# A gMLP layer rebuilt around one z2 tile, a spatial weight in four quarters and hand-over of memory tile by tile

## The chip, the cores and the metric

The kernel runs on one core of one Trainium2 chip. The metric is the device time of one execution in microseconds (us); every quoted time is the median of several executions, and a profiled execution gives the trace from which all durations below are read. TensorE does the matrix products, VectorE, ScalarE and GpSimd the element-wise work, and SyncE's queue (SP) most of the transfers.

## The reference, cut to what matters

Four layers follow each other: attention (A), gMLP (B), attention, gMLP. The change concerns B alone.

```
S, D, F = 2048, 576, 4608;  Fh = F // 2 = 2304
z  = gelu(x @ w_in)                    # x: layer-normalised, w_in: D x F
z1 = z[..., :Fh]
z2 = layernorm(z[..., Fh:])            # over the 2304 columns of a row
g  = w_sp @ z2 + b_sp[:, None]         # w_sp: S x S, mixes the rows
y  = (z1 * g) @ w_out                  # w_out: Fh x D
x  = x + y
```

The product with `w_sp` is the large one: 2048 x 2048 x 2304 in each of the two gMLP layers.

## The kernel before

A gMLP layer has three stages. The first ("z2 loop") goes through 16 blocks of 128 rows: matmuls, GELU on ScalarE, the sums for the layer norm, the normalisation into `z2b`. The second ("gates") goes through 18 half blocks of 128 columns: z1 and its GELU, then 64 matmuls with the spatial weight, then bias and product on VectorE. The third ("output product") multiplies by `w_out`. In the attention layers ahead of it, a prefetch brings three of the five row groups of `w_in`.

```
zu: z2b = [zu.tile([P, NS, 256], bf16, tag="zu", bufs=NB + 1) for b in range(NB)]   # NB = 9
wp: W_sb = wp.tile([P, NS, S], bf16)
# --- z2 loop, p1 = pool of this stage
for c in range(NPF, 5): dma(win2b[...], B_w_in[c...], eng=(nc.sync, nc.scalar)[c % 2])  # NPF = 3
def p1_main(i):
    zp = p1.tile([P, Fh], bf16, name="zp", bufs=2)
    z_full(range(2), range(4)); z_half(range(nu))          # 5 units; all row groups of w_in
    ...                                                    # units 2 to 4
    ...  # GELU with sums; squares: 1536 columns VectorE, 768 ScalarE; small statistics
    nc.gpsimd.tensor_tensor(out=rstd, in0=rstd, in1=neg_half, op=ALU.pow)
def p1_norm(i):
    for b in range(NB):                                    # one instruction per 256 columns
        if b >= NB - 3: nc.gpsimd.tensor_scalar(out=z2b[b][:, i, :], ...)
        else:           nc.vector.tensor_scalar(out=z2b[b][:, i, :], ...)
...  # spatial weight: 16 transposing transfers into W_sb, from the third block on
# --- gates: p2 opened when p1 is closed
for jj in range(NB):
    ...  # w1 loaded; z1 (20 matmuls, GELU), then per quarter q: 16 matmuls, two VectorE ops
# --- output product: p3 opened when p2 and wp are closed
wout_b = p3.tile([P, NJ - NJA, D], bf16)                   # NJA: 0 first layer, 9 last layer
for j in range(NJA, NJ): dma(wout_b[:, j - NJA, :], ...)
...  # last layer: f32 sums, GpSimd cast to bf16, one transfer per row block
```

A pool's memory, once closed, is given to the next pool. In the kernel before, the first use of the new pool's memory waits until the whole old pool is done with.

The softmax here doesn't subtract the row's maximum and nothing guards it: scores larger than these inputs give would overflow.

Of the kernel before, what the change touches and what calls it, by code (L numbers as in the profile page):

```python
# [10 lines left out]
ACT = mybir.ActivationFunctionType  # L11
# [8 lines left out]
P = 128  # L20
D = 576
# [40 lines left out]
class K:  # L62
# [24 lines left out]
    def setup(self):  # L87
# [5 lines left out]
        self.ident = c.tile([P, P], bf16, name="ident")  # L93
        make_identity(nc, self.ident[:])
# [32 lines left out]
    def open_ps(self, name):  # L127
        if self.ps_cm is not None:
            self.ps_cm.__exit__(None, None, None)
        self.ps_cm = self.tc.tile_pool(name=name, bufs=1, space=PSUM)  # L130
        self.ps = self.ps_cm.__enter__()
# [124 lines left out]
    def layer_A(self, li):  # L256
# [5 lines left out]
        do_W = False  # L262
# [129 lines left out]
        def PG(d, qk, cc, use_L=False, in_steps=False):  # L392
# [49 lines left out]
            return f  # L442

        w_state = {}
        w_rr = [0]

        def WLOAD(tt):
            def f():
                ws = sb.tile([P, S], bf16, name="ws", tag="ws", bufs=2)
                self.dma(ws[:], self.B_w_sp[tt * P:(tt + 1) * P, :], eng=nc.gpsimd)  # L450
                wt = sb.tile([P, NS, P], bf16, name="wt", tag="wt", bufs=2)
                w_state[tt] = (ws, wt)
            return f

        def WU(tt, i0):
            def f():
                ws, wt = w_state[tt]
                n = min(8, NS - i0)
                tp = self.PT_tile([P, 8, P], bf16, "w_tp")
                for ii in range(n):  # L460
                    nc.tensor.transpose(tp[:, ii, :], ws[:, (i0 + ii) * P:(i0 + ii + 1) * P], self.ident[:])
                w_rr[0] += 1
                self.copy_bf16(wt[:, i0:i0 + n, :], tp[:, :n, :], eng=("dve" if w_rr[0] % 2 == 0 else "act"))
                if i0 + 8 >= NS:
                    self.dma(self.Wd[tt], wt[:].rearrange("p a b -> p (a b)"), eng=nc.gpsimd)
            return f
# [197 lines left out]
        if do_W:  # L664
            units = []
            for tt in range(NS):
                units.append(WLOAD(tt))
                units.extend([WU(tt, i0) for i0 in range(0, NS, 8)])
            spread(units, min(LATE_STEP, NSTEP - 2), NSTEP - 1, table)

# [77 lines left out]
    def layer_B(self, li):  # L748
        nc, tc, cfg = self.nc, self.tc, self.cfg
        S, NS, Fh, NJ, NB, NQ = cfg.S, cfg.NS, cfg.Fh, cfg.NJ, cfg.NB, cfg.NQ  # L750
        x_prev = self.xres[li - 1]
        self.open_ps(f"B{li}_ps")

        zu_cm = tc.tile_pool(name=f"B{li}_zu", bufs=1)
        zu = zu_cm.__enter__()
        z2b = [zu.tile([P, NS, 256], bf16, name=f"z2b{b}", tag="zu", bufs=NB + 1) for b in range(NB)]
        wp_cm = tc.tile_pool(name=f"B{li}_W", bufs=1)
        wp = wp_cm.__enter__()
        W_sb = wp.tile([P, NS, S], bf16, name="W_sb")

        p1_cm = tc.tile_pool(name=f"B{li}_p1", bufs=2)
# [14 lines left out]
        def load_W():  # L776
            for i in range(NS):
                nc.sync.dma_start_transpose(out=W_sb[:, i, :], in_=self.B_w_sp[:, i * P:(i + 1) * P])
# [8 lines left out]
        NPOOL_NORM = min(3, NB - 1)  # L787
        zst = {}

        def p1_main(i):  # L790
            zp = p1.tile([P, Fh], bf16, name="zp", bufs=2)
            sums = p1.tile([P, ncch + 2], f32, name="z_sums", bufs=3)
            pzvs = []
            for ci, (c0, cn) in enumerate(cchunks):
                if cn > 512:
                    pz = self.H_tile("pz")
                    pzvs.append(pz[:].rearrange("p a b -> p (a b)"))
                else:
                    pz = self.PT_tile([P, 512], f32, "pzs")
                    pzvs.append(pz[:, :])  # L800
            units = []
            for ci, (c0, cn) in enumerate(cchunks):
                nsub = (cn + 511) // 512
                for sub in range(nsub):
                    w = min(512, cn - sub * 512)
                    units.append((ci, c0, sub, w))
            def z_full(us, cs):
                for u in us:
                    ci, c0, sub, w = units[u]
                    for c in cs:  # L810
                        nc.tensor.matmul(pzvs[ci][:, sub * 512:sub * 512 + w],
                                         lhsT=self.xnT[:, c, PADL + i * P:PADL + (i + 1) * P],
                                         rhs=win2(c)[:, c0 + sub * 512:c0 + sub * 512 + w],
                                         start=(c == 0), stop=False)

            def z_half(us):
                for u in us:
                    ci, c0, sub, w = units[u]
                    r = 64 * (u % 2)
                    nc.tensor.matmul(pzvs[ci][:, sub * 512:sub * 512 + w],  # L820
                                     lhsT=self.xnT[r:r + 64, 4, PADL + i * P:PADL + (i + 1) * P],
                                     rhs=win2(4)[r:r + 64, c0 + sub * 512:c0 + sub * 512 + w],
                                     start=(u >= 2), stop=(u < 2), tile_position=(r, 0))
            nu = len(units)
            z_full(range(2), range(4))
            z_half(range(nu))
            for u in range(2, nu):
                ci, c0, sub, w = units[u]
                for c in range(4):
                    nc.tensor.matmul(pzvs[ci][:, sub * 512:sub * 512 + w],  # L830
                                     lhsT=self.xnT[:, c, PADL + i * P:PADL + (i + 1) * P],
                                     rhs=win2(c)[:, c0 + sub * 512:c0 + sub * 512 + w],
                                     start=False, stop=(c == 3))
# [3 lines left out]
            junkD = p1.tile([P, SQ_D], bf16, name="z_junkD", bufs=1)  # L837
            nc.vector.tensor_tensor_reduce(out=junkD[:], in0=zp[:, 0:SQ_D], in1=zp[:, 0:SQ_D], scale=1.0,  # L838
                                           scalar=0.0, op0=ALU.mult, op1=ALU.add, accum_out=sums[:, ncch:ncch + 1])
            junkA = p1.tile([P, Fh - SQ_D], bf16, name="z_junkA", bufs=1)  # L840
            nc.scalar.activation(out=junkA[:], in_=zp[:, SQ_D:Fh], func=ACT.Square,
# [18 lines left out]
        def p1_norm(i):  # L860
            zp, mean, rstd, nmr = zst.pop(i)
            for b in range(NB):
                if b >= NB - NPOOL_NORM:
                    nc.gpsimd.tensor_scalar(out=z2b[b][:, i, :], in0=zp[:, b * 256:(b + 1) * 256], scalar1=rstd[:, 0:1],  # L864
                                            scalar2=nmr[:, 0:1], op0=ALU.mult, op1=ALU.add)
                else:
                    nc.vector.tensor_scalar(out=z2b[b][:, i, :], in0=zp[:, b * 256:(b + 1) * 256], scalar1=mean[:, 0:1],  # L867
                                            scalar2=rstd[:, 0:1], op0=ALU.subtract, op1=ALU.mult)

        for i in range(NS):  # L870
            self.run_deferred(upto_row=(i + 1) * P)
            p1_main(i)
            if i == 0:
                self.run_deferred()
            if i == min(2, NS - 1):
                load_W()
            if i >= 1:
                p1_norm(i - 1)
# [7 lines left out]
        NJA = NJ // 2 if not next_is_A else 0  # L886
        wv_ = self.B_w_out.rearrange("(j p) n -> p j n", p=P)
        R_cm = None
        wout_a = None
        if NJA > 0:  # L890
            R_cm = tc.tile_pool(name=f"B{li}_R", bufs=1, side="right")
            R = R_cm.__enter__()
            wout_a = R.tile([P, NJA, D], bf16, name="wout_a")
            self.dma(wout_a[:], wv_[:, 0:NJA, :], eng=nc.scalar)
        p2_cm = tc.tile_pool(name=f"B{li}_p2", bufs=2)
        p2 = p2_cm.__enter__()
        bsp = p2.tile([P, S], bf16, name="bsp", bufs=1)
        self.dma(bsp[:], self.B_b_sp.partition_broadcast(P), eng=nc.gpsimd)
        uT = []
        for jj in range(NB):  # L900
            w1 = p2.tile([P, 5, 256], bf16, name="w1")
            self.dma(w1[64:128, 4, :], self.B_w_in[512:576, jj * 256:(jj + 1) * 256], eng=nc.sync)
            for c in range(5):
                kc = 128 if c < 4 else 64
                self.dma(w1[:kc, c, :], self.B_w_in[c * P:c * P + kc, jj * 256:(jj + 1) * 256], eng=nc.sync)
            u = zu.tile([P, 2, S], bf16, name=f"uT{jj}", tag="zu", bufs=NB + 1)
            uT.append(u)
            for sub in range(2):
                z1T = p2.tile([P, S], bf16, name="z1T")
                pz1s = [self.H_tile("pz1") for _ in range(NQ // 2)]  # L910

                def z1_full(q, first):
                    for c in range(4):
                        nc.tensor.matmul(pz1s[q // 2][:, q % 2, :], lhsT=w1[:, c, sub * P:(sub + 1) * P],  # L914
# [10 lines left out]
                for q in range(NQ):  # L925
                    z1_half(q, q >= 2)
# [159 lines left out]
```

## Time and profile before

| | before |
|---|---|
| time, median of 4 runs | 1346.24 us (1342.95 to 1347.73) |
| span of the profiled run | 1341.8 us |
| attention, first / second | 193.1 / 156.3 us |
| z2 loop, first / second layer | 87.5 / 87.6 us |
| gates | 329.7 / 324.6 us |
| output product | 80.9 / 74.4 us |
| from the last output matmul to the end | 7.7 us |

The stages are cut where the timeline of TensorE shows the first matmul of the next stage, so a wait for the first matmul counts to the stage ahead of it.

The page of the kernel before, part 1, gives busy time, share of the span and count of instructions by engine:

```profile
PE 1243.5 (93%) x8656; PEld 636.1 (47%) x8656; DVE 614.1 (46%) x1400; ACT 391.4 (29%) x622; POOL 362.6 (27%) x508
```

TensorE is the busy engine. In the gates it is never short of work: the chain of waits shows 64 matmuls in 13.81 us, again and again. So what can be won lies between the stages and in the z2 loop.

In the z2 loop of the first gMLP layer, the groups by form (line, engine, operation, output and inputs, shape, count; busy us, mean ns; idle us before and its releaser) read so over 60 us or 12 blocks:

```profile
L864 POOL TENSOR_SCALAR z2b<-zp,z_rstd,z_nmr 128x256 bf16<-128x256 bf16 x36 | 40.0, 1121 | 1.2
L867 DVE TENSOR_SCALAR z2b<-zp,z_mean,z_rstd 128x256 bf16<-128x256 bf16 x72 | 21.5, 370 | 8.0 <-POOL z_rstd L854 8.0
L838 DVE CUSTOM_DVE_ANT_0 z_junkD<-zp 128x1536 bf16<-128x1536 bf16 x12 | 21.2, 1770 | 0.0
```

and the waits in the same loop (who waited for whom; us in total, times, longest):

```profile
ACT zp L835 <- POOL z2b L864: 16.8, 11, 1.6
DVE z2b L867 <- POOL z_rstd L854: 6.7, 10, 0.7
PE pz L811 <- ACT zp L835: 1.9, 9, 0.2
```

Six normalisations take VectorE 1.8 us per block (21.5/12), the squares 1.77, and it waits 0.7 for GpSimd's power; with the small statistics that closes a ring (a chain of waits that comes back to its start) of 5.01 us, the period of the loop. ScalarE waits too, for GpSimd's three normalisations, and TensorE a little for ScalarE.

The first z2 block, from TensorE's timeline (start, us, engine, line, what; in brackets the idle time before and what ended it):

```profile
193.13 1.44 PE L811 MATMUL pz<-win2a,xnT 128*128 128x512 bf16 x3 [0.54 <-DVE x_new L584]
197.07 0.58 PE L811 MATMUL pz<-win2b,xnT 128*128 128x512 bf16 x1 [2.50 <-DMA win2b<-in_B_w_in_dram]
...
200.69 1.01 PE L820 MATMUL pz<-win2b,xnT 64*128 64x512 bf16 x2 [1.32 <-DMA win2b<-in_B_w_in_dram]
```

and the windows (start:end, length, busy us of each engine with counts, then the granted TensorE clock, the share of the DMA engines and GB/s):

```profile
193.00:197.00 4.00, 1.44 (x3) 0.41 (x3) 0.87 (x4) 0.00 (x0) 3.47 (x4) 0.50 0.84 228
201.00:205.00 4.00, 4.00 (x11) 1.12 (x10) 0.00 (x0) 2.15 (x2) 0.00 (x0) 0.50 0.67 150
```

The block waits twice for the rest of `w_in`, and even where TensorE is 100% busy (201 to 205) its clock is 0.50: 11 matmuls in 4 us.

The start of the first output product, on the same timeline:

```profile
599.81 8.15 PE L935 MATMUL pg<-W_sb,z2b 128*128 128x512 bf16 x37
610.29 0.40 PE L972 MATMUL po<-wout_b,uT 128*128 128x288 bf16 x2 [2.32 <-DMA wout_b<-in_B_w_out_dram]
611.64 1.84 PE L972 MATMUL po<-wout_b,uT 128*128 128x288 bf16 x7 [0.95 <-DMA wout_b<-in_B_w_out_dram]
615.38 1.12 PE L972 MATMUL po<-wout_b,uT 128*128 128x288 bf16 x4 [1.89 <-DMA wout_b<-in_B_w_out_dram]
```

`w_out` is asked for when the gates are done, and TensorE follows its arrival piece by piece. The window of four of these microseconds, with the columns as above, shows the clock:

```profile
612.00:616.00 4.00, 2.11 (x10) 1.16 (x8) 0.00 (x0) 0.00 (x0) 1.15 (x3) 0.50 1.04 352
```

### The profile page before, as it was taken

To read this page: it belongs to the slowest core of one execution; us is meant where nothing else is said; L and a number is where in the kernel's file an instruction comes from. 1 tells how busy PE (TensorE), PEld (TensorE's weight loads), DVE (VectorE), ACT (ScalarE), POOL (GpSimd) and SP (SyncE) were. 2 spreads that over 40 slices of the span, in tenths; PEclk is the share of its full clock that TensorE was granted. 3 is DMA by queue.
4 is the path that set the end of the run, shared out by engine and by line. 5 is a ranking of instruction groups with operands and counts; after the bars stand their busy time and mean duration, and the time that the engine had idled before them with its cause. 6 is when DMAs were issued, how large, how long until landed. Compare 5 with 4: busy or idle time off the path is not lost. (4 is left out here: it accounts for less than half of the span.)

```text
span 1341.8 us, 21436 instructions
## 1 busy us (share of the span) xinstructions
PE 1243.5 (93%) x8656; PEld 636.1 (47%) x8656; DVE 614.1 (46%) x1400; ACT 391.4 (29%) x622; POOL 362.6 (27%) x508
## 2 busy tenths in 40 slices
PE   1999879999999999998999988799999999999997
PEld 0456644434444444445764555344444444444576
DVE  4367866862332332323434888488333233332221
ACT  3466626731111101110235665366111111001000
POOL 6427566850000000002132566588000000000111
PEclk9999989999999999997999999799999999999999
DMA  9438669220000000007652677970200000000232
GB/s 258 89 78 153 112 143 208 44 89 10 11 10 11 10 10 11 0 0 234 185 146 68 139 146 143 186 149 24 62 10 10 10 11 3 8 10 1 71 115 67
DMA packets 181728, 102.22 MB, mean 76 GB/s; under 512 B 138596, under 2 KB 163684, under 8 KB 181628
## 3 DMA queue, kind: packets, MB, share of 16 engines
q1 hardware_dynamic: 171648, 84.74, 28.1%
q10 hardware_dynamic: 6524, 9.14, 2.4%
q0 software_dynamic: 3456, 6.96, 2.2%
q8 instruction: 68, 1.11, 0.4%
q14 instruction: 32, 0.26, 0.1%
HBM read 42.34 MB, written 16.52 MB: 44 GB/s over the span
## 5 line engine op out<-in xcount | busy, mean ns | idle before, releaser
L935 PE MATMUL pg<-W_sb,z2b 128*128 128x512 bf16 x2304 | 505.8, 380 | 2.2 <-DVE z2b L867 2.2
L935 PEld LDWEIGHTS <-z2b 128*128 128x128 bf16 x2304 | 226.1, 98 | 274.6 <-DVE z2b L867 2.7
L939 DVE TENSOR_TENSOR g_tmp<-pg,bsp 128x512 f32<-128x512 f32 x144 | 99.3, 692 | 427.2 <-PE pg L935 415.9
L930 ACT ACTIVATE z1T<-pz 128x1024 bf16<-128x1024 f32 x72 | 73.7, 1024 | 547.5 <-PE pz L920 512.7
L76 POOL DMA_DIRECT2D wout_b<-in_B_w_out_dram x14 | 7.6, 548 | 635.1 <-PE pg L935 635.1
L914 PE MATMUL pz<-xnT,w 128*128 128x512 bf16 x576 | 136.9, 380 | 2.6 <-DMA w<-in_B_w_in_dram 2.6
L972 PEld LDWEIGHTS <-uT 128*128 128x128 bf16 x1152 | 114.4, 99 | 42.9 <-issue 10.6
L412 PE MATMUL pp<-xnT,wqk_sb 128*128 128x512 bf16 x400 | 102.1, 396 | 30.7 <-DMA xnT<-ln_xn 29.1
L972 PE MATMUL po<-wout_b,uT 128*128 128x288 bf16 x864 | 117.2, 293 | 9.4 <-DMA wout_b<-in_B_w_out_dram 9.4
L940 DVE TENSOR_TENSOR uT<-g_tmp,z1T 128x512 bf16<-128x512 f32 x144 | 99.5, 692 | 14.7 <-ACT z1T L930 4.8
L864 POOL TENSOR_SCALAR z2b<-zp,z_rstd,z_nmr 128x256 bf16<-128x256 bf16 x96 | 103.7, 1091 | 3.6 <-POOL z_nmr L856 0.4
L180 POOL TENSOR_SCALAR ln_xn<-x_new,ln_mv,ln_rstd 112x576 bf16<-112x576 f32 (+1 forms) x38 | 95.7, 2518 | 3.9
L914 PEld LDWEIGHTS <-w 128*128 128x128 bf16 x576 | 53.4, 98 | 77.9 <-issue 17.8
L527 DVE TENSOR_TENSOR P_sb<-P_sb,mask_base 128x1792 bf16<-128x1792 bf16 (+1 forms) x76 | 81.1, 1067 | 12.9 <-ACT P_sb L508 12.7
L505 ACT ACTIVATE P_sb<-L_ps 128x896 bf16<-128x896 f32 (+1 forms) x88 | 74.1, 870 | 35.9 <-PE O_ps L540 17.4
L835 ACT ACTIVATE zp<-pz 128x1024 bf16<-128x1024 f32 x64 | 65.0, 1021 | 47.9 <-POOL z2b L864 42.8
L162 POOL TENSOR_TENSOR ln_rstd<-ln_rstd,neg_half 112x1 f32<-112x1 f32 (+2 forms) x70 | 42.3, 605 | 134.2 <-DVE ln_rstd L161 131.4
L980 DVE TENSOR_TENSOR x_new<-po,xo 128x288 f32<-128x288 f32 x64 | 28.8, 456 | 103.6 <-PE po L972 103.6
L412 PEld LDWEIGHTS <-wqk_sb 128*128 128x128 bf16 x400 | 37.1, 100 | 72.6 <-issue 37.9
L838 DVE CUSTOM_DVE_ANT_0 z_junkD<-zp 128x1536 bf16<-128x1536 bf16 x32 | 56.8, 1774 | 26.8 <-ACT zp L835 26.8
L582 PE MATMUL pw<-wo_sb,oT 128*128 128x288 bf16 x380 | 58.9, 300 | 10.5 <-DMA oT<-o_t 8.7
L867 DVE TENSOR_SCALAR z2b<-zp,z_mean,z_rstd 128x256 bf16<-128x256 bf16 x192 | 57.4, 370 | 21.6 <-POOL z_rstd L854 21.6
(80 smaller groups left out, 1211.0 us busy)
## 6 DMA issues: line engine op xcount, KB each, us to landing
xo<-xres SPq DMA_DIRECT2D x32, 288.0 KB
xres<-x_new SPq DMA_DIRECT2D x36, 252.0 KB
w<-in_B_w_in_dram SPq DMA_DIRECT2D x72, 64.0 KB
xres<-x_new SPq DMA_DIRECT2D x16, 288.0 KB
xo<-xres SPq DMA_DIRECT2D x18, 252.0 KB
QK<-stg POOLq DMA_DIRECT2D x52, 72.0 KB, 3.7
win2a<-in_B_w_in_dram SPq DMA_DIRECT2D x2, 1728.0 KB
QK<-stg SPq DMA_DIRECT2D x48, 72.0 KB
```

What stands on the lines that cost most here:

```text
L180: e.tensor_scalar(out=xn[:nrows, 0:D], in0=x_t[:nrows, :], scalar1=mv[:nrows, 0:1], scalar2=rstd[:nrows, 0:1], op0=ALU.subtract, op1=ALU.mult)
L412: nc.tensor.matmul(pp[:, :], lhsT=wqk_sb[:, c, wc0:wc0 + P], rhs=self.xnT[:, c, col0:col0 + 512], start=(c == 0), stop=(c == 4))
L505: nc.scalar.activation(out=P_sb[:nk, 2 * hh:2 * hh + 2, :, 0:nq], in_=Lv[:nk, 2 * hh:2 * hh + 2, :, 0:nq], func=ACT.Exp, scale=float(scale))
L527: nc.vector.tensor_tensor(out=Pv[:nk, :, 0:nq], in0=Pv[:nk, :, 0:nq], in1=m[:nk, None, 0:nq].to_broadcast([nk, 16, nq]), op=ALU.mult)
L835: nc.scalar.activation(out=zp[:, c0:c0 + cn], in_=pzvs[ci][:, 0:cn], func=ACT.Gelu_apprx_tanh, accum_out=sums[:, ci:ci + 1])
L864: nc.gpsimd.tensor_scalar(out=z2b[b][:, i, :], in0=zp[:, b * 256:(b + 1) * 256], scalar1=rstd[:, 0:1], scalar2=nmr[:, 0:1], op0=ALU.mult, ...
L914: nc.tensor.matmul(pz1s[q // 2][:, q % 2, :], lhsT=w1[:, c, sub * P:(sub + 1) * P], rhs=self.xnT[:, c, PADL + q * 512:PADL + (q + 1) * 512 ...
L930: nc.scalar.activation(out=z1T[:, q2 * 512:(q2 + 2) * 512], in_=pz1s[q2 // 2][:, :, :].rearrange("p a b -> p (a b)"), func=ACT.Gelu_apprx_ ...
L935: nc.tensor.matmul(pg[:, :], lhsT=z2b[jj][:, i, sub * P:(sub + 1) * P], rhs=W_sb[:, i, q * 512:(q + 1) * 512], start=(i == 0), stop=(i == ...
L939: nc.vector.tensor_tensor(out=tmp[:], in0=pg[:, :], in1=bsp[:, q * 512:(q + 1) * 512], op=ALU.add)
L940: nc.vector.tensor_tensor(out=u[:, sub, q * 512:(q + 1) * 512], in0=tmp[:], in1=z1T[:, q * 512:(q + 1) * 512], op=ALU.mult)
L972: nc.tensor.matmul(acc[hh], lhsT=uT[j // 2][:, j % 2, i * P:(i + 1) * P], rhs=wout_j(j)[:, hh * 288:(hh + 1) * 288], start=(j == 0), stop= ...
```

## The change

The intent: free memory earlier and use it earlier. All z2 blocks and the gate results lie in one tile `Z` of ten slots; the result of block jj goes into the slot that block jj-1 left (the spare tenth slot takes the squares that nobody reads, then the first result). With the blocks in one tile, VectorE normalises eight of them in one instruction and GpSimd one. z gets three buffers. The spatial weight is four tiles, and the last block computes its gates quarter by quarter, so that the quarters come free one after the other and `w_out` can be loaded over them. Pools of the gMLP layer and of PSUM are opened with `reuse_waits="tile"`: a new tile waits for the old tiles that it overlaps, not for their whole pool. The first z2 block does the three prefetched row groups first. The last layer stores bf16 halves straight from VectorE.

```diff
-        z2b = [zu.tile([P, NS, 256], bf16, name=f"z2b{b}", tag="zu", bufs=NB + 1) for b in range(NB)]
+        def pool(name, bufs=1):
+            return tc.tile_pool(name=f"B{li}_{name}", bufs=bufs, reuse_waits="tile")
+        Z = zu_cm.__enter__().tile([P, NB + 1, NS, 256], bf16, name="Z")
+        spare = Z[:, NB].rearrange("p a b -> p (a b)")
+        def uT(jj):
+            return Z[:, NB if jj == 0 else jj - 1]...
-        W_sb = wp.tile([P, NS, S], bf16, name="W_sb")
+        Wq = [wp.tile([P, NS, 512], bf16, name=f"Wq{q}") for q in range(NQ)]
...
-            zp = p1.tile([P, Fh], bf16, name="zp", bufs=2)
+            zp = p1.tile([P, Fh], bf16, name="zp", bufs=3)
...
+            if i == 0:          # first block: prefetched row groups of all units, then the rest
+                ...
...
-            for b in range(NB):  # one instruction per block, three of them on GpSimd
-                ...
+            nb = NB - 1
+            nc.vector.tensor_scalar(out=Z[:, 0:nb, i, :], in0=zv[:, 0:nb, :], scalar1=mean[:, 0:1],
+                                    scalar2=rstd[:, 0:1], op0=ALU.subtract, op1=ALU.mult)
+            nc.gpsimd.tensor_scalar(out=Z[:, nb, i, :], in0=zv[:, nb, :], scalar1=rstd[:, 0:1], ...)
...
+            else:                                   # last block of the gates
+                z1(jj, 0)
+                z1(jj, 1)
                 for q in range(NQ):
+                    for sub in range(2):
+                        gate(jj, sub, q)
...
-        wout_b = p3.tile([P, NJ - NJA, D], bf16, name="wout_b", bufs=1)
-        for j in range(NJA, NJ):
-            self.dma(wout_b[:, j - NJA, :], wv_[:, j, :], eng=(nc.sync, nc.gpsimd)[j % 2])
+        wouts = [p3.tile([P, NJH, D], bf16, name=f"wout{h_}", bufs=1) for h_ in range(2)]
+        for h_ in range(2):
+            self.dma(wouts[h_][:], wv_[:, h_ * NJH:(h_ + 1) * NJH, :], eng=nc.gpsimd)
...
+                if last:
+                    self.dma(self.out[i * P:(i + 1) * P, hs], x_new[:, hs], eng=(nc.sync, nc.scalar)[hh])
```

Also gone are an identity matrix and a weight transposition that was never used; the spatial weight comes in 4 transposing transfers in place of 16. Three more edits touch the seams and are cut above: `w1` comes in three transfers in place of six and is asked for one block ahead; the first and the last block of the gates compute both halves of z1 before their gates; and the last layer no longer loads half of `w_out` early (`wout_a`).

## The prediction

> **What bounds the kernel now.** TensorE: 1243.5 of 1341.8 us busy (93%, page part 1). About 650 us are the gating products, 64 matmuls in 13.8 us per half block (chain of waits), at a granted clock of 1.00 with nothing waiting. The change leaves them alone. What can be won lies in the two gMLP layers, at four seams.
>
> 1. *z2 loop* (15 iterations after the first). 5.01 us each (timeline), while TensorE's own work fits in 4.43 (one early iteration ran so). The ring is VectorE: 6 normalisations of 256 columns 1.79, sum of squares 1.77, small statistics 0.93, wait for GpSimd's power 0.67 (waits), sum about 5.0 with starts overlapping. ScalarE also waits 1.6 for GpSimd's three normalisations (3.33 us), with two z buffers.
>  Change: one VectorE instruction for 8 blocks, one block on GpSimd, three z buffers. The 256-column instruction took 0.335 us at best[...] TensorE sets about 4.5-4.6. Gain 0.4 x 15 x 2 = about 11 us. [...]
>
> 2. *First z2 iteration.* 13.6 and 13.8 us (timeline, 193.1-206.7 and 847.5-861.3), against 4.4 later: waits for the upper rows of w_in of 2.5+1.3 and 3.1+0.9 us, nearly all at clock 0.50 (windows). [...] The new order does prefetched rows first: about 13.5 matmul slots, 5.8 us at half clock, cover the wait. Expect about 8 us: gain 5.5 x 2 = 11. Tile-wise waits may start the load earlier.
>
> 3. *z2 to gates.* About 3 and 2 us idle while w1 (issued only after the last normalisation) lands. Tile-wise waits let it start when w_in is last read. Gain about 4 us, if TensorE's queue has gate products ahead of z1.
>
> 4. *Gates to w_out.* First layer: 607.96 to 690.64 = 82.7 us for 576 matmuls that take 70.5 at full clock; lost 12.1 us (idle plus clock 0.50 until about 625). Last layer: 74.3, lost 3.8. New: w_out goes into quarters of the spatial weight freed 20.7 and 13.8 us before the gates end (six and four groups of 3.45); 2.65 MB at the 330 GB/s seen there is 8 us. Gain about 15.
>
> 5. *Rest.* Output stored in bf16 without the 0.67 us cast; PSUM handed over per tile (0.5 us waits): about 1.5.
>
> Sum about 42 us. DMA transposes keep their bytes and finish long before need. **Predicted 1304 us, range 1293 to 1322; faster 0.88, same 0.10, slower 0.02.**
>
> **What would show it.** z2 period near 4.5 and no ScalarE wait on z2b; [...] first iteration about 8 us; no TensorE wait on w_out and clock 1.00 at the start of the output product; the gates' 13.8 us unchanged.
>
> **What would make it wrong.** [...] TensorE queue order with z1 first, waiting for w1 (5 us per layer); false dependences inside the one big z2 tile, stalling gates on VectorE; w_out on GpSimd's queue issued late.

The sum is 11 + 11 + 4 + 15 + 1.5 = 42.5, "about 42 us", and the predicted time is the 1346 of the kernel before less that. The first 11 us rest on the estimate that the loop would come down to TensorE's own 4.5 to 4.6 us, from the 4.43 of one iteration. For the second term the trace of the kernel before shows a granted clock of 0.50 from 190 to 205 us, and the 5.8 us of 13.5 matmuls fit it: at 0.50, four matmuls over 512 columns took 1.68 us (856.99 to 858.67, in the second layer), 0.42 each. That the block would then take about 8 us is an estimate too.

## The result, and the profile after

The kernel after takes 1298.84 us (median of 4 runs, 1296.28 to 1300.92) against 1346.24 of the kernel before in the same rounds. The ratio is 0.965, with a 95% interval of 0.962 to 0.968. Ratios here and below are the mean time of one kernel's fast runs over that of the other's of the same rounds, so they are not quite the ratio of the medians quoted. The predicted time was 1304.0, the range 1293 to 1322.

| stage | before | after | difference |
|---|---|---|---|
| attention, first | 193.1 | 193.5 | +0.3 |
| z2 loop | 87.5 | 75.8 | -11.7 |
| gates | 329.7 | 323.5 | -6.2 |
| output product | 80.9 | 70.6 | -10.3 |
| attention, second | 156.3 | 159.4 | +3.1 |
| z2 loop | 87.6 | 74.7 | -12.9 |
| gates | 324.6 | 323.5 | -1.1 |
| output product | 74.4 | 70.7 | -3.7 |
| end | 7.7 | 3.2 | -4.5 |
| span | 1341.8 | 1294.8 | -47.0 |

Every stage of the gMLP layers became shorter, and the attention layers, whose code is the same but for the waits of their PSUM pool, did not. The page's part 1 of the kernel after:

```profile
PE 1215.6 (94%) x8529; PEld 632.8 (49%) x8656; DVE 584.3 (45%) x1240; ACT 393.8 (30%) x622; POOL 282.7 (22%) x416
```

The share of TensorE hardly moved, 93 to 94%, while the time fell by 3.5%: of the 47.0 us saved, up to 27.9 had been counted as busy, for matmuls at half clock count too (4.00 of 4.00 us busy at 0.50 in the window from 201 to 205 above). (The page of the kernel after lacks 127 matmul records, so its busy time is somewhat low.)

The groups of the z2 loop after, by form, over the 52 us from 210 to 262:

```profile
L806 DVE CUSTOM_DVE_ANT_0 Z<-zp 128x1536 bf16<-128x1536 bf16 x12 | 21.7, 1812 | 5.2 <-ACT zp L804 5.2
L831 DVE TENSOR_SCALAR Z<-zp,z_mean,z_rstd 128x2048 bf16<-128x2048 bf16 x12 | 9.8, 813 | 8.0 <-POOL z_rstd L821 8.0
L833 POOL TENSOR_SCALAR Z<-zp,z_rstd,z_nmr 128x256 bf16<-128x256 bf16 x12 | 9.7, 805 | 1.2
```

and its waits, over the same 50 us from 215 to 265 as before:

```profile
ACT zp L804 <- PE pz L777: 10.8, 11, 1.0
DVE Z L831 <- POOL z_rstd L821: 7.4, 11, 0.7
DVE Z L806 <- ACT zp L804: 5.2, 10, 0.6
```

One instruction over 2048 columns takes 0.813 us where six over 256 took 1.8. VectorE now waits for ScalarE, ScalarE for TensorE, and nobody holds TensorE: its row, the third one before, is gone from the table. The period, read from the starts of the squares, is 4.64 us.

The first z2 block and its clock:

```profile
193.46 3.28 PE L777 MATMUL pz<-win2a,xnT 128*128 128x512 bf16 x11 [0.22 <-issue]
196.58 0.49 PE L777 MATMUL pzs<-win2a,xnT 128*128 128x256 bf16 x3
196.90 1.03 PE L777 MATMUL pz<-win2b,xnT 128*128 128x512 bf16 x4
197.77 0.27 PE L777 MATMUL pzs<-win2b,xnT 128*128 128x256 bf16 x1
198.78 0.61 PE L777 MATMUL pz<-win2b,xnT 64*128 64x512 bf16 x4 [0.74 <-DMA win2b<-in_B_w_in_dram]
```

```profile
193.00:197.00 4.00, 3.78 (x16) 1.83 (x16) 1.29 (x5) 0.00 (x0) 2.69 (x4) 0.76 0.34 62
201.00:205.00 4.00, 3.95 (x20) 1.53 (x20) 2.55 (x8) 3.48 (x12) 0.61 (x2) 1.00 1.22 249
```

The prefetched row groups cover the wait, all but 0.74 us of it, and the granted clock is back at 1.00 within the block: 0.52 from 194 to 195, 1.00 from 195 to 197 and in the window from 201 to 205, where it was 0.50 before.

The start of the first output product after:

```profile
581.74 11.17 PE L895 MATMUL pg<-Wq,Z 128*128 128x512 bf16 x50
592.74 9.47 PE L951 MATMUL po<-wout,Z 128*128 128x288 bf16 x76
```

No wait is left at that seam. The clock differs too: the granted clock is 0.50 from 612 to 624 in the kernel before, where TensorE waited again and again for `w_out`, and 1.00 throughout that product in the kernel after.

### The profile page after: what moved, and what is told of

Read it like the earlier page. It is cut to its first block, busy times and chain, and to the rows that moved or that the text cites. A ratio compares the mean times of both kernels' runs of the same rounds, so it can differ in the third digit from the quotient of the medians.

```text
span 1294.8 us, 20985 instructions
## 1 busy us (share of the span) xinstructions
PE 1215.6 (94%) x8529; PEld 632.8 (49%) x8656; DVE 584.3 (45%) x1240; ACT 393.8 (30%) x622; POOL 282.7 (22%) x416
## 4 chain that ended last, share of the span: by engine, by line
PE 76%; POOL 10%; issue 6%; DMA 4%; DVE 2%; ACT 2%; SPq 0%; ACTq 0%; POOLq 0%; DVEq 0%
PE pg L895 38%; PE pz L877 11%; PE po L951 11%; PE pz L777 10%; POOL ln_xn L177 7%; PE pp L408 4%; POOL ln_rstd L159 2%; DMA xnT<-ln_xn 1%; PE pzs L777 1%; ACT P_sb L480 1%; DMA QK<-stg 1%; POOL ln_xn L179 1%; PE pv L366 1%; DMA win2b<-in_B_w_in_dram 1%; DVE P_sb L499 1%
## 5 line engine op out<-in xcount | busy, mean ns | idle before, releaser
L895 PE MATMUL pg<-Wq,Z 128*128 128x512 bf16 x2254 | 500.2, 379 | 4.4 <-DVE Z L831 1.9
L895 PEld LDWEIGHTS <-Z 128*128 128x128 bf16 x2304 | 224.9, 98 | 274.2 <-DVE Z L831 2.9
L877 PE MATMUL pz<-xnT,w 128*128 128x512 bf16 (+1 forms) x708 | 151.4, 380 | 1.4 <-issue 0.9
L951 PE MATMUL po<-wout,Z 128*128 128x288 bf16 x1152 | 141.4, 286 | 0.0
L408 PE MATMUL pp<-xnT,wqk_sb 128*128 128x512 bf16 x373 | 99.3, 398 | 31.6 <-DMA xnT<-ln_xn 28.6
L951 PEld LDWEIGHTS <-Z 128*128 128x128 bf16 x1152 | 112.7, 98 | 28.8
L777 PEld LDWEIGHTS <-xnT 128*128 128x128 bf16 (+1 forms) x800 | 67.1, 98 | 84.7 <-issue 26.9
L900 DVE TENSOR_TENSOR Z<-g_tmp,z1T 128x512 bf16<-128x512 f32 x144 | 99.6, 692 | 10.0 <-DVE g_tmp L899 0.5
L777 PE MATMUL pz<-win2a,xnT 128*128 128x512 bf16 x370 | 102.9, 383 | 1.2 <-issue 0.4
L877 PEld LDWEIGHTS <-w 128*128 128x128 bf16 (+1 forms) x720 | 57.4, 97 | 90.1 <-issue 30.5
L554 PE MATMUL pw<-wo_sb,oT 128*128 128x288 bf16 x380 | 59.3, 301 | 14.5 <-DMA oT<-o_t 12.7
L806 DVE CUSTOM_DVE_ANT_0 Z<-zp 128x1536 bf16<-128x1536 bf16 x32 | 57.4, 1793 | 27.1 <-ACT zp L804 27.1
L961 DVE TENSOR_TENSOR x_new<-po,xo 128x288 f32<-128x288 f32 (+1 forms) x64 | 28.8, 456 | 87.8 <-PE po L951 87.8
```

The costliest lines, as they stand in the source:

```text
L408: nc.tensor.matmul(pp[:, :], lhsT=wqk_sb[:, c, wc0:wc0 + P], rhs=self.xnT[:, c, col0:col0 + 512], start=(c == 0), stop=(c == 4))
L777: nc.tensor.matmul(pzvs[ci][:, sub * 512:sub * 512 + w], lhsT=self.xnT[r0:r1, c, PADL + i * P:PADL + (i + 1) * P], rhs=win2(c)[r0:r1, c0 + ...
L877: nc.tensor.matmul(pz1s[q // 2][:, q % 2, :], lhsT=w1[r0:r1, c, sub * P:(sub + 1) * P], rhs=self.xnT[r0:r1, c, PADL + q * 512:PADL + (q + ...
L895: nc.tensor.matmul(pg[:, :], lhsT=Z[:, jj, i, sub * P:(sub + 1) * P], rhs=Wq[q][:, i, :], start=(i == 0), stop=(i == NS - 1))
L900: nc.vector.tensor_tensor(out=uT(jj)[:, sub, qs], in0=tmp[:], in1=z1Ts[jj, sub][:, qs], op=ALU.mult)
L951: nc.tensor.matmul(acc[hh], lhsT=uT(j // 2)[:, j % 2, i * P:(i + 1) * P], rhs=wouts[j // NJH][:, j % NJH, hh * 288:(hh + 1) * 288], start= ...
```

## The experiments

Twelve kernels were run. All were correct. Each changes the kernel after in the one way shown, and is compared with it stage by stage. The instruction order of every engine is the same as in the kernel after for `e3_two_z`, `e4_p3_pool`, `e7_p1_pool` and `e8_p2_pool`; in the others it is not. Two cautions hold for all of them. The four runs of the kernel after lie in two pairs, at 1296.3 and 1296.8 and at 1300.9 and 1300.9 us, so medians that differ by less than some 4 us decide nothing alone. And the times of stages come from one profiled run of each kernel: of the kernel after a fast one (1296.8), of `e1_norm_split` and `e12_warm_only` the slowest of their runs (1319.1 and 1304.2).

### What shortened the z2 loop

Theory: VectorE's own ring set the period, and the fused instruction shortens it. Rivals: the third z buffer, or the blocks taken off GpSimd.

`e1_norm_split` cuts the normalisation up again:

```diff
-            nc.vector.tensor_scalar(out=Z[:, 0:nb, i, :], in0=zv[:, 0:nb, :], ...)
-            nc.gpsimd.tensor_scalar(out=Z[:, nb, i, :], ...)
+            for b in range(NB - 3):     nc.vector.tensor_scalar(out=Z[:, b, i, :], in0=zv[:, b, :], ...)
+            for b in range(NB - 3, NB): nc.gpsimd.tensor_scalar(out=Z[:, b, i, :], in0=zv[:, b, :], ...)
```

> The kernel after, but the normalisation is cut again as before: six vector instructions of 256 columns and three GpSimd instructions per row block; the three z buffers stay. Theory (the vector engine's own ring sets the z2 loop, and the fused instruction shortens it): the loop period goes back from 4.64 to about 5.0 us, the first-to-gates stretch grows by about 0.37 x 15 = 5.5 us per gMLP layer, the whole by about 11 us (about 1310 us, ratio to before about 0.973). Rival (the third z buffer is what freed the loop, because ScalarE waited 1.6 us for GpSimd): the period stays near 4.64 and the time within 3 us of the kernel after, with no ScalarE wait on z.

Measured: 1316.01 us, ratio to before 0.977 (0.974 to 0.979). The period is 5.01 us again, in both layers. ScalarE's wait for GpSimd all but vanished (1.3 us in total from 215 to 265, 16.8 before) and the period did not care: that wait had been beside the point. The loss is about 16 us by the ratios (17 by the medians) and not 11. With three buffers TensorE runs ahead of VectorE and leaves the loop early, and the bill comes at the first gates (timeline of TensorE):

```profile
279.25 0.61 PE L897 MATMUL pg<-Wq,Z 128*128 128x512 bf16 x2 [2.53 <-DVE Z L832]
284.26 6.09 PE L897 MATMUL pg<-Wq,Z 128*128 128x512 bf16 x19 [4.41 <-DVE Z L832]
```

The gates grew by 8 us per layer (331.5 and 331.4 against 323.5). Part of the rest, 4 us in the first layer, is a wait for `w_in` that belongs to another matter (below).

`e2_fuse_six` keeps one VectorE instruction, for six blocks, and gives GpSimd its three back:

```diff
-            nb = NB - 1
+            nb = NB - 3
-            nc.gpsimd.tensor_scalar(out=Z[:, nb, i, :], ...)
+            for b in range(nb, NB): nc.gpsimd.tensor_scalar(out=Z[:, b, i, :], in0=zv[:, b, :], ...)
```

> The kernel after, but GpSimd keeps three blocks of the normalisation, and the vector engine does its six in one instruction. Theory (one instruction in place of six is what pays, its fixed cost paid once): [...] the period stays at 4.64, time within 3 us of the kernel after. Rival (taking blocks off GpSimd is what pays): the period is near 5.0 and the time about 11 us above the kernel after.

Measured: 1299.19 us, ratio 0.964 (0.962 to 0.967), period 4.64. So the number of instructions paid, not the share of GpSimd. The group line gives a second point for the cost of the fused instruction:

```profile
L831 DVE TENSOR_SCALAR Z<-zp,z_mean,z_rstd 128x1536 bf16<-128x1536 bf16 x11 | 7.5, 679 | 10.0 <-POOL z_rstd L821 10.0
```

From 1536 to 2048 columns the mean goes from 679 to 813 ns: 512 columns in 134 ns are 3.8 columns per ns. The straight line through the two points, an estimate, leaves 277 ns per instruction at zero columns and gives 344 ns at 256 columns; the mean before was 370 ns, the shortest 333. The same 1536 columns took 1.8 us in six instructions in the kernel before and 0.679 in one here.

`e3_two_z` takes the third z buffer away:

```diff
-            zp = p1.tile([P, Fh], bf16, name="zp", bufs=3)
+            zp = p1.tile([P, Fh], bf16, name="zp", bufs=2)
```

> The kernel after with two z buffers in place of three; every engine has the same instruction order. Theory: with the fused instruction the stretch from the first GELU of a block to its last normalisation is 8.0 us in the trace of after, below two periods of 4.64 = 9.3 us, so two buffers are enough: no change, within 2 us of the kernel after. Rival (the third buffer carries the gain): period near 5.0, about 10 us slower, ScalarE waits on GpSimd's normalisation again.

Measured: 1301.95 us, ratio 0.966 (0.964 to 0.968). The steady period is 4.64 us, as with three buffers; the buffer is not needed there. The z2 stretches were nevertheless 4.5 and 2.6 us longer, all of it in the first two blocks. Up to the first squares it is 2.7 and 0.9 us; in the first layer that is one wait:

```profile
200.74 0.61 PE L777 MATMUL pz<-win2b,xnT 64*128 64x512 bf16 x4 [4.01 <-DMA win2b<-in_B_w_in_dram]
```

From the first squares to the second it is 1.8 us more in each layer. In the second layer that is a wait of ScalarE for GpSimd's normalisation of the first block, whose buffer the third block needs:

```profile
837.02 0.38 ACT L804 ACTIVATE zp<-pzs 128x256 bf16<-128x256 f32 x1 [2.32 <-POOL Z L833]
```

So the third buffer pays once, at the start of the loop, and not in each period. The attention layers were 0.8 and 2.2 us shorter in that run, so part of it cancels.

### What the seam to the output product was worth

`e4_p3_pool` makes the pool of the output product wait for whole pools:

```diff
-        p3_cm = pool("p3", 2)
+        p3_cm = tc.tile_pool(name=f"B{li}_p3", bufs=2)
```

> The kernel after, but the pool of the output product waits for whole pools again, so that w_out is loaded only when all gates are done; instruction order is the same. Theory (the early load into freed quarters removes the w_out wait and the half clock behind it): TensorE waits about 9 to 10 us for the first half of w_out at the end of the gates in both layers, then runs cold for a few us; 10 to 12 us lost per layer, total about 20 to 24 us above the kernel after (more than the 16 us that the seam gained, as the last layer now has no half loaded early). Rival (the gain at this seam came from the split into two large transfers, not from their start): less than 8 us in total.

Measured: 1326.28 us, ratio 0.985 (0.982 to 0.988). TensorE's timeline:

```profile
602.13 4.12 PE L951 MATMUL po<-wout,Z 128*128 128x288 bf16 x18 [11.56 <-DMA wout<-in_B_w_out_dram]
608.37 16.90 PE L951 MATMUL po<-wout,Z 128*128 128x288 bf16 x123 [2.12 <-DMA wout<-in_B_w_out_dram]
```

Gates and output product together lose 17.4 us in the first layer and 11.2 in the last, 28.6 in all, more than the 20 to 24 expected; the first half took 11.6 us to come and not 9 to 10. The 18 matmuls behind that wait took 4.12 us, 0.23 each, against 0.12 at this place in the kernel after (76 in 9.47). The two large transfers without the early start are worse than the small ones of the kernel before. So the early start is what pays.

`e5_last_order` lets the last block run its gates half by half, as the others do:

```diff
-                for q in range(NQ):
-                    for sub in range(2):
+                for sub in range(2):
+                    for q in range(NQ):
                         gate(jj, sub, q)
```

> The kernel after, but the last 256-column block runs its gates half by half as all the others, not quarter by quarter, so the first quarter of the spatial weight comes free about 10 us (three groups of 3.45 us) before the end instead of 20.7, the second about 7 us before. Theory: the first half of w_out (1.3 MB, 7.8 us to land in the trace of after) still arrives in time, the second half lands about 1 to 3 us after the gates end, of which the first nine matmuls hide 1 us; 0 to 3 us lost per layer at this seam, nothing elsewhere. Rival (quarter order is what makes the early load possible): 8 us or more lost per layer.

Measured: 1300.39 us (2 runs), ratio 0.966 (0.964 to 0.968). The output products take 71.39 and 71.62 us against 70.56 and 70.72: 0.8 and 0.9 us. So the special order of the last block is worth about 2 us of the 47. Whether the four quarters themselves are needed, no run with one weight tile shows.

### What the first z2 block was worth

`e6_first_order` gives the first block the old order of matmuls:

```diff
-            if i == 0:
+            if i < 0:
                 for u in range(2):
```

> The kernel after, but the first z2 block uses the old order of its matmuls (all rows of w_in for the first two units, then the upper rows). Theory (first-block gain is partly the order, partly the earlier load of w_in): the block waits after three matmuls for the fourth row group, stays at half clock longer, and the z2 stretch grows by 2 to 4 us per layer. If the earlier load alone gave the gain, it grows by less than 1 us; if the order alone, by 6 to 7 us.

Measured: 1309.23 us (2 runs), ratio 0.973 (0.970 to 0.975). The z2 stretches are 81.9 and 77.6 us: 6.1 and 2.9 us longer, 9.0 in all. One layer shows what was written for "the order alone", the other what was written for both; the expectation does not hold for the first layer.

`e7_p1_pool` makes the pool of the z2 loop wait for whole pools, so that the rest of `w_in` is asked for as late as before:

```diff
-        p1_cm = pool("p1", 2)
+        p1_cm = tc.tile_pool(name=f"B{li}_p1", bufs=2)
```

> The kernel after, but the pool of the z2 loop waits for whole pools, so that w_in's upper rows are asked for only after the last attention projection, as before; same instruction order. Theory (the earlier load collides with the last transposing transfers of the attention layer: in the trace of after the last projection waited 2.9 and 1.9 us for its transposed operand, before 0.2 and 1.2): the attention stretches get shorter by 0.5 to 3 us each, the z2 stretches longer by 1 to 3 us each, the whole within 3 us of the kernel after. Rival (no collision): attention unchanged and z2 longer, 4 us or more slower in all.

Measured: 1304.88 us, ratio 0.969 (0.968 to 0.971). The z2 stretches are 6.0 and 5.2 us longer, the attention stretches 2.0 and 0.7 shorter: in the trace 8.4 us slower, in the medians 6. The net figure of the expectation (within 3 us) was wrong; the early load is worth more than I thought. But the collision it names is there. The last attention projection needs an operand that a transposing transfer brings. In `e7_p1_pool`, SP's queue issues it at 186.75 and TensorE uses it at 189.06:

```profile
186.75 1.17 SPq L540 DMA_TRANSPOSE oT<-o_t  x1
189.06 2.58 PE L554 MATMUL pw<-wo_sb,oT 128*128 128x288 bf16 x10 [0.25 <-DMA oT<-o_t]
```

In the kernel after, with the load of `w_in` from ScalarE's queue (ACTq) ahead of it, it is issued at 186.70 and used at 190.66:

```profile
185.39 5.10 ACTq L75 DMA_DIRECT2D win2b<-in_B_w_in_dram  x2
186.70 1.19 SPq L540 DMA_TRANSPOSE oT<-o_t  x1
190.66 2.58 PE L554 MATMUL pw<-wo_sb,oT 128*128 128x288 bf16 x10 [1.87 <-DMA oT<-o_t]
```

The same transfer took 2.31 us from issue to use in one case (also 2.31 in the kernel before) and 3.96 in the other. In the second attention layer the figures are 2.36 before and 4.31 after. Only the pair of transfers on ScalarE's queue comes earlier in the kernel after: the third piece, in SP's queue, is issued at 194.82, and in `e7_p1_pool` at 194.90.

All the kept traces, two layers each, show when the two collide. The transposing transfer is used 2.3 to 2.4 us after its issue where the load is issued only later (kernel before and `e7_p1_pool`), and also where the load was issued 2.8 to 3.8 us before it (first layer of `e1_norm_split` and `e3_two_z`, second of `e10_warm`). It takes 3.8 to 6.2 us in the other 21 cases, where the load was issued 1.0 to 1.6 us before it. So the delay goes with the moment of issue, and that differs from run to run.

### The seam from z2 to the gates

`e8_p2_pool` does the same to the pool of the gates, so that `w1` is loaded only after the last normalisation:

```diff
-        p2_cm = pool("p2", 2)
+        p2_cm = tc.tile_pool(name=f"B{li}_p2", bufs=2)
```

> The kernel after, but the pool of the gates waits for whole pools, so that w1 is asked for only after the last normalisation, as before; same instruction order. Theory: w1 lands about 5 us later (it was asked for 5 us earlier, at 269.9 against 275); in after it is first used at 277.9, so TensorE waits about 1 to 3 us per layer at the first z1 product; 2 to 6 us in all. If the time is unchanged, the fused normalisation alone closed this seam.

Measured: 1301.07 us (2 runs), ratio 0.967 (0.965 to 0.969). The gates take 324.47 and 325.45 us against 323.50: 1.0 and 2.0 us, 2.9 in all, of the 4.9 us that this seam gained. How the other 2 us divide between the shorter normalisation, the fewer transfers of `w1` and the new order of z1 is not shown.

### The end of the kernel

`e11_tail` brings the old store back:

```diff
-            x_new = p3.tile([P, D], bf16 if last else f32, name="x_new3", bufs=3)
+            x_new = p3.tile([P, D], f32, name="x_new3", bufs=3)
-                if last:
-                    self.dma(self.out[i * P:(i + 1) * P, hs], x_new[:, hs], eng=(nc.sync, nc.scalar)[hh])
+            if last:
+                ob = p3.tile([P, D], bf16, name="ob", bufs=2)
+                nc.gpsimd.tensor_copy(out=ob[:], in_=x_new[:])
+                self.dma(self.out[i * P:(i + 1) * P, :], ob[:])
```

> The kernel after with the old store of the output: f32 sums, a GpSimd cast, one transfer per row block on one queue. The end of the kernel, from the last output matmul on, took 7.7 us before and 3.2 after. Theory of the prediction (only the cast of 0.67 us and its hand-over count): the tail grows by about 0.7 to 1.2 us. Rival (the store's size and queue or the tail's waits make the whole difference): the tail grows by 4 us or more.

Measured: 1302.43 us, ratio 0.966 (0.962 to 0.971); in the trace the end takes 6.9 us against 3.2, so 3.7 us hang on the store, and neither figure of the theory holds. The cast is 0.67 us of it. The waits of SP's queue in the last 8 us, in `e11_tail` and then in the kernel after, seem to show where most of the rest is:

```profile
SPq L1064 <- PEq L1064: 3.4, 2, 3.0
SPq L1062 <- PEq L1062: 0.7, 2, 0.5
```

At the very end SP waits 3.0 us with the old store and 0.5 with the new; the kernel before showed 3.5. The table puts this down to the sequencer of TensorE (PEq), but the releaser in such a table is inferred. The instructions at the last line of the program (count; shortest, median and longest in ns; first and last start in us) point to another cause. They are, of GpSimd's sequencer (POOLq), in the kernel before, in `e11_tail` and in the kernel after:

```profile
L1081 POOLq DRAIN  x3: 46/102/6327, 1334.7 to 1341.6; - x3
L1064 POOLq DRAIN  x3: 46/102/5510, 1294.5 to 1300.5; - x3
L1062 POOLq DRAIN  x2: 46/74/102, 1294.2 to 1294.5; - x2
```

In the kernel before all engines have such records at this line. In `e11_tail` GpSimd's begins at 1294.5, with the last cast, and lasts 5.51 us, to 1300.0. SP's first DRAIN begins at 1297.1, TensorE's had ended at 1293.9, and the next instruction of SP starts at 1300.1. The kernel before shows the same with 6.33 us. The kernel after has no work of GpSimd at the end, and no DRAIN of it longer than 0.10 us there (its long one, 12.38 us, starts at 1207.6, with the last transfer of `w_out`). So some 2.8 of the 3.7 us go with GpSimd's DRAIN, by the times at which it and SP's wait end; what a DRAIN waits for, and why this one outlasts the cast of 0.67 us by so much, is not shown by any run.

### Attempts to do better

`e9_four_ahead` prefetches four row groups of `w_in`, to shrink the colliding load:

```diff
-    NPF = 3
+    NPF = 4
-        XG = 4
+        XG = 3
-            self.dma(win2b[:kc, c - NPF, :], ..., eng=(nc.sync, nc.scalar)[c % 2])
+            self.dma(win2b[:kc, c - NPF, :], ..., eng=nc.scalar)
```

> An attempt to do better: the kernel after, with four row groups of w_in prefetched in place of three (room for it by loading the first input in groups of three row blocks, not four), and the rest of w_in on ScalarE's queue. Theory (the early load of w_in delays the last transposing transfer, whose result was used 3.96 us after its issue in after and 2.31 us in e7): half of the bytes are left to collide, so the last projection waits 1 to 1.6 us less, and the first z2 block no longer waits for w_in (0.7 us); 2 to 4 us faster than the kernel after over two layers. Rival (the delay has another source than those bytes): attention stretches unchanged within 0.5 us, gain under 1 us.

Measured: 1299.84 us, ratio 0.964 (0.960 to 0.968): nothing gained. The collision became worse, 5.87 us from issue to use (188.89 to 194.76) with half of the bytes of the load (of the rows on ScalarE's queue 128 are left of 192). So "fewer bytes, less delay" does not hold here. What is left comes as two transfers of 64 rows each, issued 1.2 us before the transposing one. That shape is not needed for so long a delay: in the second layer of `e4_p3_pool` the unchanged pair gave 6.24 us. The run also loads the first input in smaller groups, so its total does not test the prefetch alone.

`e10_warm` gives TensorE more to do at the end of attention and moves the load that stood in SP's queue:

```diff
-            self.dma(win2b[:kc, c - NPF, :], ..., eng=(nc.sync, nc.scalar)[c % 2])
+            self.dma(win2b[:kc, c - NPF, :], ..., eng=nc.scalar)
             else:                       # the last pieces of attention
+                if off == 4:            # ahead of an attention projection
+                    JUNK(8)()           # eight matmuls whose result nobody reads
                 fn()
```

> An attempt to do better: the kernel after, with 8 idle matmuls ahead of each of the last two attention projections (where TensorE waits 2.1 and 1.9 us for transposed operands), and all of the rest of w_in on ScalarE's queue. Theory (idle gaps at the end of attention put TensorE on half clock, 0.50 from 188 to 195 in after): the clock stays at 1.00, the projections take 1.4 in place of 2.6 us and the first z2 matmuls run at 0.22 us each; 2 to 3 us per layer, 4 to 6 us in all. Rival (the chain through the transposing transfers sets the end of attention, and z2 then waits for w_in): clock 1.00, but less than 2 us gained.

Measured: 1293.62 us (1293.36 to 1293.80, 4 runs), ratio 0.960 (0.956 to 0.963), about 5 us below the median of the kernel after and the fastest of all; the intervals of the two ratios just touch, but none of its four runs was as slow as the fastest of the kernel after (1296.28). The clock is 1.00 where it was 0.50, and the projections take 1.40 us where they took 2.58:

```profile
188.00:193.00 5.00, 3.43 (x21) 1.89 (x21) 2.29 (x8) 1.28 (x1) 3.14 (x4) 1.00 1.01 244
189.81 1.40 PE L554 MATMUL pw<-wo_sb,oT 128*128 128x288 bf16 x10 [1.51 <-DMA oT<-o_t]
```

`e12_warm_only` has the idle matmuls alone, and the load where it was:

```diff
             else:
+                if off == 4:
+                    JUNK(8)()
                 fn()
```

> The idle matmuls of e10 alone, with the loads of w_in where the kernel after has them. Theory (keeping the clock at 1.00 through the end of attention is what e10 gained): attention stretches about 191 and 157 us as in e10 (after: 193.5 and 159.4), the clock 1.00 there, about 4 us faster than the kernel after and within 3 us of e10. If moving the load to ScalarE's queue was what paid, the attention stretches are short but z2 waits 2 us or more longer per layer for w_in and the time is within 2 us of the kernel after.

Measured: 1300.19 us (5 runs, 1296.31 to 1304.15), ratio 0.966 (0.964 to 0.969): nothing gained. TensorE arrives at the z2 block at a clock of 1.00 (184 to 197) and with its first matmuls done sooner, and then stands still for the piece of `w_in` that SP's queue issues only after the attention layer's own transfers:

```profile
196.20 0.60 SPq L75 DMA_DIRECT2D win2b<-in_B_w_in_dram  x1
200.19 1.04 PE L779 MATMUL pz<-win2b,xnT 64*128 64x512 bf16 x4 [3.08 <-DMA win2b<-in_B_w_in_dram]
```

In the second layer the wait is 2.2 us, and in both layers the clock fell back to 0.50 by the end of it (from 199.5 and 831.0). In `e10_warm` the same piece was on ScalarE's queue, and the waits for it were none in the first layer and 1.4 us in the second. So the idle matmuls alone do not give the gain of `e10_warm`. The move alone was not tried: whether it needs the idle matmuls is not shown.

## Why the prediction was right

The time and the range hold. The mechanisms held at three of the five places (1, 3 and 4); at the first block the size came out by a cause of which only half was foreseen, and the rest is two errors that cancel. Sizes are from the profiled spans.

1. *z2 loop, predicted 11 us.* Right in cause and size. The period went from 5.01 to 4.64, 0.37 x 15 x 2 = 11.1 us. The fused instruction took 0.813 us (the estimate of it is cut from the record: it rested on a rate that no trace had shown); `e1_norm_split` and `e2_fuse_six` show that it alone did it, and `e3_two_z` that the third buffer is needed only at its start. One step was misread: "TensorE's own work fits in 4.43 (one early iteration ran so)". That block had some of its small matmuls done ahead of it (256-column units stand at 860.99 and 861.20 in the trace, before the block's start at 861.32). With no one holding TensorE, the steady loop takes 4.64.

2. *First block, predicted 11 us.* Near in size, but in part by luck. The z2 stretches shrank by 24.6 us in all, and less the 11.1 of the loop that leaves 13.5. Without the new order they lose 9.0 (`e6_first_order`), without the earlier load 11.2 (`e7_p1_pool`). So, by one trace each, the load alone is worth some 13.5 - 9.0 = 4.5 us and the order alone 13.5 - 11.2 = 2.3: each needs the other. I had booked all of it on the order ("about 13.5 matmul slots, 5.8 us at half clock, cover the wait"), and the earlier load only as something that "may" help. With the order and the late load, `e7_p1_pool` still waits for the rest of `w_in` in the first layer, by 1.80 and 2.25 us.

3. *z2 to gates, predicted 4 us.* 3.9 us in the first layer (280.61 to 607.96 before, 269.24 to 592.74 after) and 1.1 in the second, 4.9 in all. The worry that TensorE's queue would have z1 first was unfounded: gate products stand first in it (in the kernel after from 269.24, z1 from 277.91).

4. *Gates to output product, predicted 15 us.* From the end of the gates, 12.7 us in the first layer (607.96 to 691.19 before, 592.74 to 663.30 after) and 3.7 in the last, 16.4 in all. `e4_p3_pool` shows the cause: the start of the load, not its cut into two transfers.

5. *Rest, predicted 1.5 us.* This sum came out near its size by two errors that cancel. "Output stored in bf16 without the 0.67 us cast" was mis-sized: the end became 4.5 us shorter, of which `e11_tail` gives 3.7 back, some 2.8 of it with GpSimd's DRAIN of 5.51 us, which the prediction did not know of. The shorter PSUM waits that it names here were not tested alone. And the prediction had no term for the attention layers, which grew by 0.3 and 3.1 us. `e7_p1_pool` shows a cost of the earlier load there, of 1.65 us on the last transposing transfer of the first attention layer, and stretches shorter by 2.0 and 0.7 us without it. In the second attention layer the transfer takes 1.95 us longer (4.31 against 2.36). Another 1.5 us of its 3.1 is lost before the load is issued at 814.44: from 754.7 to 758.2 the granted clock is 0.50 there (1.00 in the kernel before), and by 761.2 the projections are 1.5 us behind. What starts that stretch is not shown; it comes in some runs and not in others, and across the twelve runs the layer took 156.2 to 160.5 us.

None of the fears came true: the fused instruction took 0.813 us where the six took 1.8 (the fear of a longer one is among the cuts), the one big tile made no false waits (the gates' 323.5 us are the lowest of both kernels), and GpSimd's queue issued `w_out` in time (at 572.49 and 579.39 in the first layer, whose gates end at 592.74).

## What to carry to other kernels

When one engine is nearly saturated, look at the seams between stages, and count what a seam costs from its start until the TensorE clock is back at 1.00; here 6 us of idle time, the waits for `w_out` in the first layer, cost 12. Count short instructions over neighbouring tiles, and lay tiles out so that one instruction can cover them: here 1536 columns took 1.8 us in six and 0.679 in one. An earlier load is not free: ask which transfer it will now run beside (here a transposing transfer took 3.96 us from issue to use in place of 2.31) and what stands ahead of it in its queue (with the idle matmuls in both runs, a piece of `w_in` was waited for by 3.1 and 2.2 us on SP's queue, by 0 and 1.4 on ScalarE's), and test clock and load apart and together: here the idle matmuls alone gained nothing. And look at what each engine still has open at the end of the kernel: here a DRAIN of 5.51 us that began with a cast of 0.67.
